# Attention, soft MoE and a gated FFN on one core: the beginning in another order, one streamed weight as two tiles, U and its input in two PSUM banks each

## The chip, the cores and the metric

The kernel runs on one core of a Trainium2 chip. The metric is the device time of one execution in microseconds (us). Three runs of the kernel before gave a median of 526.25 us (526.21 to 527.63).

## The reference

Three layers stand behind each other. The numbers: 4 batches, 8 heads, 768 positions, head width 64; then 3072 tokens of width 512; 8 experts of 4 slots and 1024 hidden units; a last layer of 2048 hidden units.

```python
scores = scale * np.matmul(q, k.transpose(0, 1, 3, 2))
keep = is_global | is_local                     # first n_global keys, and the n_local keys before a position
scores = np.where(keep, scores - slope * dist, -1e9)
x = softmax(scores) @ v                         # tokens (3072, 512)

logits = x @ phi                                # 32 slots
slot_input = softmax(logits, axis=0).T @ x
slot_out[e] = np.maximum(slot_input[e] @ w1[e], 0) @ w2[e]
x = softmax(logits, axis=1) @ slot_out

r = np.maximum(x @ w_in, 0.0)
out = (r * r) @ w_out
```

`n_local` (96) and `n_global` (8) are inputs of the kernel, so the masks are made on the chip.

## The kernel before

Attention goes over 48 units, each a batch, a pair of 128-row query tiles (`tp`, 0 to 2) and a pair of heads (`pr`). A unit i passes through stages that are issued for different units side by side, in an order written out by hand; every engine runs its own instructions in that order. `stage_qk` (L217) makes the scores on TensorE into two PSUM banks (tag `s`, four banks, so two units at once). `stage_max` (L229) adds the mask and takes the row minimum of the negated scores on VectorE. `stage_exp` (L248) is the exponential on ScalarE. `stage_T` (L257) transposes on TensorE, `stage_ev` (L268) copies the transposed block out of PSUM on VectorE or ScalarE, `stage_pv` (L273) multiplies with the values and `stage_x` (L291) copies the result. From unit 4 on a `route` step by step makes the router's logits with `phib`.

A unit's loads are issued on SyncE's queue: `load_qk` (L102) brings 6 blocks of 128 columns (384 KB: two of queries, two of keys, two of the keys that each tile also sees), `load_v` (L108) 4 blocks (256 KB). SyncE issues in program order and waits at a load until the buffer that it overwrites is free, so a load behind it waits as well. The first unit of a batch (`tp` 0) does not use one of the two last blocks: its first tile sees no earlier keys.

The masks are made at the start (L114 to L164). Two tables, R2 (row minus column) and J (column), come as `cmask` from the constants. `n_i`, the two numbers of the input, comes on ScalarE's queue; `n_1` is it as float (L137), a product with `one` spreads it over the partitions (`n_p`, L140), and from that VectorE and GpSimd make `dist` and eight masks, mask h for head h: VectorE mask 0, ScalarE mask 1, GpSimd masks 2 to 7, one after the other. `warm(n, ...)` (L76) is n products of zeros or constants whose result nobody reads.

All weights of the experts together do not fit beside attention. Nine of them are loaded during attention (slots `p0` to `p8`); when attention's buffers are released (L743), the pool `stream` takes their place, with slots `s0`, `s1`, `s2` of 16 KB a partition each. The first streamed weight is `w2_1` in `s0`. Attention's pool `att` gives its first 16 KB a partition to the four `raw` buffers (3 KB each) and then the two `va` buffers (2 KB each, values of half of the units); these make up `s0`. A block named "last" (L753) ends the routing and writes `slotZ`. Then eight times `w1_of` (L805), eight times `w2_of` (L908), with the conversion of the last layer's first weights beside it on VectorE and ScalarE.

Between the experts and the last layer lies a short chain (L1077 to L1101). The slots' result is copied out (`SO`), turned (`pst`), copied in two halves (`soT`: ScalarE the first, VectorE the second), and multiplied with the last layer's first 256 columns (`f0`) in two chunks of 128 (`pu`); each chunk is copied by ScalarE and corrected by VectorE into `U0`. `gemm1` (L997) multiplies U with the spread router shares, and squares; `gemm2` (L1017) makes the output, in five passes over 12 blocks of tokens, with sums kept in `oacc` (in `s0`, `p5`, `p7`).

Of the kernel before, what the change touches and what calls it, by code (L numbers as in the profile page):

```python
# [34 lines left out]
C_ID, C_SI4, C_R2, C_J = 0, 128, 256, 384  # L35
C_W = 512
# [4 lines left out]
def attention_moe_ffn(ctx: ExitStack, tc, qk, vx, nn, phi, w1, w2, w_in, w_out, consts, relw, out):  # L41
# [10 lines left out]
    con = full("con", [P, C_R2])  # L52
# [49 lines left out]
    def load_qk(i):  # L102
        b, tp, pr = units[i]
        r = early.pop("raw", None) if i == 0 else raw_tile(i)
        nc.sync.dma_start(r, qk[b, tp, pr])
        raws[i] = r

    def load_v(i):  # L108
        b, tp, pr = units[i]
        v = early.pop("v", None) if i == 0 else v_tile(i)  # L110
        nc.sync.dma_start(v, vx[b, tp, pr])
        vals[i] = v

    early = {"raw": raw_tile(0), "v": v_tile(0)}  # L114
    cmask = att.tile([P, C_W - C_R2], F32, tag="sm", name="cmask", bufs=3)
    nc.sync.dma_start(cmask, consts[:, C_R2:C_W])
# [3 lines left out]
    nc.sync.dma_start(con, consts[:, 0:C_R2])  # L120
    load_v(0)
    load_qk(2)
    load_qk(3)
# [4 lines left out]
    J = cmask[:, P : 2 * P]  # L128
    mtmp = post.tile([P, 6, P], F32, tag="xb", name="mtmp")
# [4 lines left out]
    V.tensor_tensor(own, own, R2, op=ALU.max)  # L134
    G.tensor_scalar(R1, R2, float(P), None, op0=ALU.add)

    V.tensor_copy(n_1, n_i)  # L137
    warm(10, zero, idle)
    n_p = aps.tile([P, 512], F32, tag="m", name="n_p", bufs=4)
    nc.tensor.matmul(n_p[:, 0:4], lhsT=one, rhs=n_1, start=True, stop=True)  # L140
    V.tensor_copy(n_f, n_p[:, 0:4])
# [16 lines left out]
    for h in range(H):  # L158
        m = mk.tile([P, 3, P], BF16, tag=f"mask{h}", name=f"mask{h}")
        if h == 1:  # L160
            nc.scalar.activation(m, dist, AF.Copy, scale=slope8(h))
        else:
            (G if h else V).tensor_scalar(m, dist, slope8(h), None, op0=ALU.mult)
        masks.append(m)  # L164
# [31 lines left out]
    def load_w(i, part=0, parts=1):  # L196
        name, src, shape, dt = items[i]
        if name == first[0][0]:

            t = slot(SLOTS[i], [P, 2, shape[1]], dt, "raw_0")  # L200
            for j in range(2):
                wt[first[j][0]] = t[:, j, :]
        elif part == 0 and name != first[1][0]:
            wt[name] = slot(SLOTS[i], shape, dt, name)
        n = shape[1] // parts
        ps = slice(part * n, part * n + n)
        nc.sync.dma_start(wt[name][:, ps], src[:, ps])
# [9 lines left out]
    def stage_qk(i):  # L217
        b, tp, pr = units[i]
        r = raws.pop(i)
        sc = [aps.tile([P, 2, 2, P], F32, tag="s", name=f"s{i}_{hh}", bufs=4) for hh in range(2)]  # L220
        for tt in range(2):
            n = width(tp, tt)
            for hh in range(2):
                r0 = hh * D
                rhs = r[r0 : r0 + D, 2 + tt : 3 + tt, :] if n == 1 else r[r0 : r0 + D, 2 + tt : 6 : 2, :]
                nc.tensor.matmul(sc[hh][:, tt, 0:n, :], lhsT=r[r0 : r0 + D, tt, :], rhs=rhs, start=True, stop=True)  # L226
        st[i] = [sc]
# [45 lines left out]
    def stage_pv(i):  # L273
        b, tp, pr = units[i]
        v = vals.pop(i)
        pT = st[i][1]
        o = aps.tile([P, 2, P], F32, tag="s" if i == NU - 1 else "m", name=f"o{i}", bufs=4)
        for tt in range(2):
            n = width(tp, tt)
            for c in range(n):  # L280
                for hh in range(2):
                    nc.tensor.matmul(o[hh * D : hh * D + D, tt, :], lhsT=v[:, tt + 2 * c, hh * D : hh * D + D],  # L282
                                     rhs=pT[:, 2 * tt + hh, c, :], start=c == 0, stop=c == n - 1)
        st[i] = o
# [212 lines left out]
    nc.sync.dma_start(phib, phi)  # L497
# [3 lines left out]
    warm(5, zero, idle)  # L501
# [3 lines left out]
    stage_exp(0, 1)  # L505
    stage_max(1, 0)
    stage_max(1, 1)
    warm(4, zero, idle)
# [4 lines left out]
    for i in range(2):  # L513
        if i:
            stage_T(i)
            stage_max(i + 2, 0)
            stage_ev(i, 0, V.tensor_copy)
        else:
            stage_ev(i, 0, V.tensor_copy)
            stage_max(i + 2, 0)  # L520
        if i:
            stage_exp(i + 1, 0)
            stage_x(i - 1)
        stage_ev(i, 1, nc.scalar.copy)
        stage_exp(i + 1, 1)
        stage_qk(i + 3)
        stage_max(i + 2, 1)
        load_qk(i + 6)
        load_v(i + 3)
        stage_pv(i)  # L530
    stage_exp(3, 0)
# [221 lines left out]
    with tc.block(name="last"):  # L753
# [26 lines left out]
        for c in halves:  # L780
            for h in halves:
                kc = 2 * h + c
                R = slice(2 * h * NS, 2 * h * NS + 2 * NS)
                nc.tensor.matmul(pv[h][:, kc * NS : kc * NS + NS], lhsT=ps[R, c * P : c * P + P], rhs=sden[R], start=False, stop=c == 1)
        for h, eng in ((0, V.tensor_copy), (1, nc.scalar.copy)):
            eng(z[:, :, 2 * h : 2 * h + 2, 0:4], pv[h][:, 2 * h * NS : 2 * h * NS + 2 * NS].rearrange("p (k e s) -> p e k s", e=E, s=4))
# [121 lines left out]
    def w2_of(e):  # L908
        c = wt[f"w2_{e}"]
        for fc in range(8):  # L910
            g = fc % 4
            z = e * 8 * NS + fc * NS
            nc.tensor.matmul(pSO[g * NS : g * NS + NS, :], lhsT=hZ[:, z : z + NS], rhs=c[:, fc, :],  # L913
                             start=e == 0 and fc < 4, stop=e == E - 1 and fc >= 4)
# [82 lines left out]
    def gemm1(q, n, j):  # L997
# [7 lines left out]
        for k in range(K):  # L1005
            c0 = (2 * j + k) * P
            nc.tensor.matmul(ph[:, k, :], lhsT=U[:, c0 : c0 + P], rhs=cst[:, n * TB : n * TB + TB], start=True, stop=True)  # L1007
        rg = ex.tile([P, 2, 2, TB], F32, tag="e", name=f"rg{q}_{n}_{j}", bufs=2)
# [8 lines left out]
    def gemm2(q, n, m):  # L1017
# [7 lines left out]
        o = oacc[k // 8][:, k % 8, :]  # L1025
# [54 lines left out]
    pst = bps.tile([P, 512], F32, tag="sel", name="pst")  # L1080
    pu = bps.tile([P, 512], F32, tag="pu", name="pu0")
# [5 lines left out]
    for kc in range(4):  # L1087
        nc.tensor.matmul(pst[:, kc * P : kc * P + P], lhsT=SO[:, kc * P : kc * P + P], rhs=si4, start=True, stop=True)
    nc.scalar.copy(soT[:, 0:2, :].rearrange("p k s -> p (k s)"), pst[:, 0 : 2 * P])
    V.tensor_copy(soT[:, 2:4, :].rearrange("p k s -> p (k s)"), pst[:, 2 * P : 4 * P])  # L1090
# [5 lines left out]
    for c0 in range(0, WIDTHS[0], P):  # L1096
        c = slice(c0, c0 + P)
        for kc in range(4):
            nc.tensor.matmul(pu[:, c], lhsT=soT[:, kc, :], rhs=f0[:, kc, c], start=kc == 0, stop=kc == 3)
        nc.scalar.copy(U0[:, c], pu[:, c])  # L1100
        V.scalar_tensor_tensor(U0[:, c], U0[:, c].bitcast(F32), odd, pu[:, c], op0=ALU.mult, op1=ALU.add)  # L1101
# [5 lines left out]
    oacc = [slot(t, [P, 8, DM], F32, f"oacc{i}") for i, t in enumerate(("s0", "p5", "p7"))]  # L1107
# [117 lines left out]
def layout(inputs):  # L1225
# [30 lines left out]
    qk = units(qt, kt, seen(kt, 4))  # L1256
    vx = units(vt, seen(vt, 3))
# [5 lines left out]
    con[:, C_R2 : C_R2 + P] = i[:, None] - i[None, :]  # L1263
    con[:, C_J : C_J + P] = i[None, :]
# [36 lines left out]
```

## Time and profile before

| what | us |
|---|---|
| median of three runs | 526.25 |
| the profiled execution | 526.89 |
| its span, first to last instruction | 525.0 |
| TensorE busy | 513.7 (98%) |
| VectorE busy | 381.8 (73%) |
| ScalarE busy | 306.6 (58%) |
| GpSimd busy | 169.1 (32%) |
| attention, to the end of the routing | 0 to about 182 |
| experts | about 182 to 217.6 |
| chain to the last layer | 217.6 to 225.1 |
| last layer | 225.1 to 525.0 |

Matmuls are pipelined in the chip and overlap in the trace, so a TensorE that is busy 98% of the time need not be at its peak: how often it starts a product tells more. An engine's idle time is put down to what ended it. A row of the timeline merges neighbours of one line, so the time of a row divided by its count is near the interval between starts.

### The profile page before, as it was taken

What the parts mean: (1) busy time and instruction counts of PE and PEld (TensorE: products, weight loads), DVE (VectorE), ACT (ScalarE), POOL (GpSimd) and SP (SyncE); (2) the same over time, 40 slices, a digit from 0 to 9 for tenths busy, and PEclk for the clock granted to TensorE, in tenths of its full rate; (3) what the DMA queues carried; (4) which work ended last, traced back from release to release, by engine and by line L of the source; (5) the groups of instructions that cost most, each with busy time, mean ns of one, the idle gap of its engine ahead of it and who ended that gap; (6) DMA issues with size and microseconds to landing.
All of it is one profiled execution on the core that took longest, in us unless ns stands there. A gap on an engine that the chain in (4) does not pass through costs nothing.

```text
span 525.0 us, 10077 instructions
## 1 busy us (share of the span) xinstructions
PE 513.7 (98%) x3628; PEld 393.5 (75%) x3628; DVE 381.8 (73%) x933; ACT 306.6 (58%) x818; POOL 169.1 (32%) x149
## 2 busy tenths in 40 slices
PE   8999999999999999999999999999999999999997
PEld 6777777677767734467787888878888888888886
DVE  5788888787887837588888997967848667445553
ACT  4987878878888303376674655545545446444441
POOL 7000000000000110044655675456554536534441
PEclk9999999999999999999999999999999999999999
DMA  8789999999992999904314030030200000002333
GB/s 292 259 264 318 361 338 311 344 345 316 315 356 70 348 374 423 384 0 162 116 45 160 1 141 21 5 117 0 90 31 1 0 2 0 1 9 113 120 121 121
DMA packets 25978, 89.19 MB, mean 170 GB/s; under 512 B 2882, under 2 KB 3522, under 8 KB 23874
## 3 DMA queue, kind: packets, MB, share of 16 engines
q1 hardware_dynamic: 25776, 88.35, 46.2%
q8 instruction: 30, 0.49, 0.4%
q14 instruction: 26, 0.21, 0.1%
q10 hardware_dynamic: 146, 0.13, 0.1%
HBM read 82.18 MB, written 6.29 MB: 169 GB/s over the span
## 4 chain that ended last, share of the span: by engine, by line
PE 52%; DVE 7%; ACT 1%; issue 1%; POOL 1%; DVEq 0%; POOLq 0%
PE acc L1029 15%; PE acc L1030 14%; PE acc L1031 14%; PE h L1007 4%; PE pSO L913 3%; DVE rg L1012 1%; DVE cvyi L924 1%; DVE cvyi L923 1%; DVE cvyo L924 1%; DVE oacc L1036 1%; PE pre L809 1%; DVE winf L927 1%; DVE oacc L1038 1%; POOL g L1015 1%; ACT rg L1011 1%
## 5 line engine op out<-in xcount | busy, mean ns | idle before, releaser
L1015 POOL TENSOR_TENSOR g<-rg,g 128x512 fp32r<-128x512 f32 (+1 forms) x109 | 135.0, 1241 | 163.5 <-DVE rg L1012 160.7
L1029 PE MATMUL acc<-w,g 128*128 128x512 f32 (+1 forms) x387 | 152.2, 393 | 1.0 <-DVE oacc L1036 1.0
L1031 PE MATMUL acc<-w,g 128*128 128x512 f32 (+1 forms) x387 | 150.6, 389 | 0.7 <-POOL g L1015 0.7
L1030 PE MATMUL acc<-w,g 128*128 128x512 f32 (+1 forms) x387 | 151.3, 391 | 0.0
L1011 ACT ACTIVATE rg<-h 128x512 f32<-128x512 f32 (+1 forms) x109 | 59.6, 546 | 121.9 <-PE h L1007 115.7
L1038 DVE TENSOR_TENSOR oacc<-acc,oacc 128x512 f32<-128x512 f32 x95 | 65.2, 687 | 58.8 <-PE acc L1031 58.8
L254 ACT ACTIVATE sm<-sm,nm 128x256 f32<-128x256 f32 (+1 forms) x192 | 92.8, 489 | 0.3 <-DVE nm L239 0.3
L1031 PEld LDWEIGHTS acc<-w,g 128*128 128x128 f32 x387 | 72.7, 188 | 18.3 <-POOL g L1015 2.8
L1029 PEld LDWEIGHTS acc<-w,g 128*128 128x128 f32 x387 | 72.7, 188 | 17.5 <-ACT rg L1011 2.3
L1030 PEld LDWEIGHTS acc<-w,g 128*128 128x128 f32 x387 | 73.0, 189 | 11.0
L1012 DVE SCALAR_TENSOR_TENSOR rg<-h,rg 128x512 f32<-128x512 f32 (+1 forms) x109 | 67.7, 621 | 16.9 <-ACT rg L1011 16.8
L239 DVE CUSTOM_DVE_ANT_0 sm<-s,mask 128x256 f32<-128x256 f32 (+1 forms) x192 | 66.9, 396 | 3.7 <-ACT sm L254 1.5
L1014 ACT ACTIVATE g<-rg 128x512 fp32r<-128x512 f32 (+1 forms) x109 | 63.4, 582 | 3.5
L226 PE MATMUL s<-raw 64*128 64x256 f32 (+1 forms) x384 | 52.6, 395 | 0.1
L664 POOL TENSOR_TENSOR lh<-lh 128x256 f32<-128x256 f32 x1 | 0.7, 729 | 158.6 <-PE pt L265 158.6
L265 PE MATMUL pt<-con,sm 128*128 128x128 f32 x352 | 45.4, 276 | 1.6 <-ACT pT L271 1.6
L282 PE MATMUL o<-pT,v 128*64 128x128 f32 x704 | 44.4, 277 | 0.2 <-ACT pT L271 0.2
L265 PEld LDWEIGHTS pt<-con,sm 128*128 128x128 f32 x352 | 38.5, 141 | 7.0 <-ACT pT L271 2.8
L282 PEld LDWEIGHTS o<-pT,v 128*64 128x64 f32 x704 | 37.9, 137 | 7.3 <-DVE nm L239 2.2
L226 PEld LDWEIGHTS s<-raw 64*128 64x128 f32 x384 | 31.8, 194 | 14.4 <-DMA v<-in_vx 6.3
L1007 PEld LDWEIGHTS h<-cu 128*128 128x128 f32 x192 | 36.0, 188 | 8.2 <-DVE cu L1101 0.8
L1007 PE MATMUL h<-cu 128*128 128x256 f32 x192 | 40.3, 281 | 0.6 <-DVE cu L1101 0.6
(211 smaller groups left out, 544.5 us busy)
## 6 DMA issues: line engine op xcount, KB each, us to landing
w<-in_w SPq DMA_DIRECT2D x40, 512.0 KB, 6.7
raw<-in_qk SPq DMA_DIRECT2D x48, 384.0 KB, 5.7
v<-in_vx SPq DMA_DIRECT2D x48, 256.0 KB, 4.5
w<-in_w SPq DMA_DIRECT2D x6, 2048.0 KB, 10.1
out_x<-oacc SPq DMA_DIRECT2D x23, 256.0 KB, 2.0
win<-in_w_in SPq DMA_DIRECT2D x2, 2048.0 KB, 9.1
wout<-in_w_out SPq DMA_DIRECT2D x2, 2048.0 KB, 7.9
win<-in_w_in SPq DMA_DIRECT2D x2, 1536.0 KB, 7.3
```

The costliest lines, as they stand in the source:

```text
L226: nc.tensor.matmul(sc[hh][:, tt, 0:n, :], lhsT=r[r0 : r0 + D, tt, :], rhs=rhs, start=True, stop=True)
L239: V.tensor_tensor_reduce(out=sm[:, j, 0:n, :], in0=sc[hh][:, tt, 0:n, :], in1=m[:, 2:3, :] if n == 1 else m[:, 0:2, :], scale=-QK_SCALE, s ...
L254: nc.scalar.activation(sm[:, j, 0:n, :], sm[:, j, 0:n, :], AF.Exp, bias=nm[:, j : j + 1], scale=-1.0, accum_out=chunk_sums(i // NPR)[:, tt ...
L265: nc.tensor.transpose(pp[tt][:, hh, c, :], sm[:, 2 * tt + hh, c, :], ident)
L282: nc.tensor.matmul(o[hh * D : hh * D + D, tt, :], lhsT=v[:, tt + 2 * c, hh * D : hh * D + D], rhs=pT[:, 2 * tt + hh, c, :], start=c == 0, ...
L1007: nc.tensor.matmul(ph[:, k, :], lhsT=U[:, c0 : c0 + P], rhs=cst[:, n * TB : n * TB + TB], start=True, stop=True)
L1012: V.scalar_tensor_tensor(g, ph[:, k0:k1, :], 0.0, r, op0=ALU.max, op1=ALU.mult)
L1015: G.tensor_tensor(g2[:, 1, js, :], g, g2[:, 0, js, :].bitcast(F32), op=ALU.subtract)
L1029: nc.tensor.matmul(pa[:, cs], lhsT=ghi[:, j, ms], rhs=whi[:, j, cs], start=j == 0, stop=False)
L1030: nc.tensor.matmul(pa[:, cs], lhsT=ghi[:, j, ms], rhs=wlo[:, j, cs], start=False, stop=False)
L1031: nc.tensor.matmul(pa[:, cs], lhsT=glo[:, j, ms], rhs=whi[:, j, cs], start=False, stop=j == J - 1)
L1038: V.tensor_tensor(o, pa, o, op=ALU.add)
```

## The change

- The loads of a `tp` 0 unit leave out the block that it does not use: 5 of 6 and 3 of 4 blocks. On the host the last two blocks of a unit change places, so that the unused one is last; the indices in `stage_qk` and `stage_pv` follow.
- R2 and J are made by two `iota` on GpSimd in place of the load of `cmask`. The loads at the start go in the order raw 0, raw 1, raw 2, constants, raw 3, v 0, v 1; `phib` is loaded after the first two units' loop.
- `n_1` is made right after the two first VectorE instructions, 5 in place of 10 `warm` stand before the spread, 4 behind it. The 5 and the 4 `warm` around the first `stage_max` go.
- Mask 3 is made by VectorE between the maxima of unit 0 and unit 1. In the first two units VectorE copies both halves of the transposed block.
- `s0` becomes two tiles, `s0a` and `s0b`, of 8 KB a partition, each with a load of its own; `oacc` is cut in parts of 4 tokens' tiles.
- `pst` gets two banks, and `pu` one bank for each chunk. Four `warm` stand at the end of the block "last", and four between the two first products of `gemm1`.

```diff
-        nc.sync.dma_start(r, qk[b, tp, pr])
+        n = 5 if tp == 0 else 6
+        nc.sync.dma_start(r[:, 0:n], qk[b, tp, pr][:, 0:n])
...
-        nc.sync.dma_start(v, vx[b, tp, pr])
+        n = 3 if tp == 0 else 4
+        nc.sync.dma_start(v[:, 0:n], vx[b, tp, pr][:, 0:n])
...
-    cmask = att.tile([P, C_W - C_R2], F32, tag="sm", name="cmask", bufs=3)
-    nc.sync.dma_start(cmask, consts[:, C_R2:C_W])
+    cmask = att.tile([P, 2 * P], F32, tag="sm", name="cmask", bufs=3)
     load_qk(0)
     early["pT"] = pT_tile(0)
     load_qk(1)
-    nc.sync.dma_start(con, consts[:, 0:C_R2])
+    load_qk(2)
+    nc.sync.dma_start(con, consts)
+    load_qk(3)
     load_v(0)
-    load_qk(2)
-    load_qk(3)
     load_v(1)
...
+    G.iota(R2, [[-1, P]], base=0, channel_multiplier=1, allow_small_or_imprecise_dtypes=True)
+    G.iota(J, [[1, P]], base=0, channel_multiplier=0, allow_small_or_imprecise_dtypes=True)
...
     V.tensor_tensor(own, own, R2, op=ALU.max)
+    V.tensor_copy(n_1, n_i)
     G.tensor_scalar(R1, R2, float(P), None, op0=ALU.add)
-    V.tensor_copy(n_1, n_i)
-    warm(10, zero, idle)
+    warm(5, zero, idle)
     n_p = aps.tile([P, 512], F32, tag="m", name="n_p", bufs=4)
     nc.tensor.matmul(n_p[:, 0:4], lhsT=one, rhs=n_1, start=True, stop=True)
+    warm(4, zero, idle)
...
-        else:
+        elif h != 3:
             (G if h else V).tensor_scalar(m, dist, slope8(h), None, op0=ALU.mult)
...
+        elif SLOTS[i] == "s0":
+            wt[name] = [slot(f"s0{h}", [P, 4, DM], dt, f"{name}{h}") for h in "ab"]
+            for h in range(2):
+                nc.sync.dma_start(wt[name][h], src[:, 4 * h : 4 * h + 4])
+            return
...
     stage_qk(1)
-    nc.sync.dma_start(phib, phi)
...
-    warm(5, zero, idle)
     stage_max(0, 0)
     stage_exp(0, 0)
     stage_max(0, 1)
     stage_exp(0, 1)
+    V.tensor_scalar(masks[3], dist, slope8(3), None, op0=ALU.mult)
     stage_max(1, 0)
     stage_max(1, 1)
-    warm(4, zero, idle)
...
             stage_ev(i, 0, V.tensor_copy)
+            stage_ev(i, 1, V.tensor_copy)
             stage_max(i + 2, 0)
         if i:
             stage_exp(i + 1, 0)
             stage_x(i - 1)
-        stage_ev(i, 1, nc.scalar.copy)
+            stage_ev(i, 1, V.tensor_copy)
...
         stage_pv(i)
+    nc.sync.dma_start(phib, phi)
...
+        warm(4, con, idle)
         for h, eng in ((0, V.tensor_copy), (1, nc.scalar.copy)):
...
+            if q == 0 and n == 0 and k == 0:
+                warm(4, con, idle)
...
-    pst = bps.tile([P, 512], F32, tag="sel", name="pst")
-    pu = bps.tile([P, 512], F32, tag="pu", name="pu0")
+    pst = [bps.tile([P, 512], F32, tag="sel", name="pst0"), pp_of("pst1")]
+    pu = [bps.tile([P, 512], F32, tag=f"pu{j}", name=f"pu0_{j}")[:, 0:P] for j in range(WIDTHS[0] // P)]
...
-    nc.scalar.copy(soT[:, 0:2, :].rearrange("p k s -> p (k s)"), pst[:, 0 : 2 * P])
-    V.tensor_copy(soT[:, 2:4, :].rearrange("p k s -> p (k s)"), pst[:, 2 * P : 4 * P])
+    nc.scalar.copy(soT[:, 0:2, :].rearrange("p k s -> p (k s)"), pst[0][:, 0 : 2 * P])
+    V.tensor_copy(soT[:, 2:4, :].rearrange("p k s -> p (k s)"), pst[1][:, 0 : 2 * P])
...
-            nc.tensor.matmul(pu[:, c], lhsT=soT[:, kc, :], rhs=f0[:, kc, c], start=kc == 0, stop=kc == 3)
-        nc.scalar.copy(U0[:, c], pu[:, c])
-        V.scalar_tensor_tensor(U0[:, c], U0[:, c].bitcast(F32), odd, pu[:, c], op0=ALU.mult, op1=ALU.add)
+            nc.tensor.matmul(pu[c0 // P], lhsT=soT[:, kc, :], rhs=f0[:, kc, c], start=kc == 0, stop=kc == 3)
+        nc.scalar.copy(U0[:, c], pu[c0 // P])
+        V.scalar_tensor_tensor(U0[:, c], U0[:, c].bitcast(F32), odd, pu[c0 // P], op0=ALU.mult, op1=ALU.add)
...
-    oacc = [slot(t, [P, 8, DM], F32, f"oacc{i}") for i, t in enumerate(("s0", "p5", "p7"))]
+    oacc = [slot(t, [P, 4, DM], F32, f"oacc{i}") for i, t in enumerate(("s0a", "s0b"))]
+    for t in ("p5", "p7"):
+        o8 = slot(t, [P, 8, DM], F32, f"oacc_{t}")
+        oacc += [o8[:, 0:4, :], o8[:, 4:8, :]]
```

## Rows read from the trace of the kernel before

**Rows 1.** Windows by stage: busy us and count per engine, PEclk, DMA share, GB/s

```profile
25.00:160.00 135.00, 133.23 (x1453) 100.37 (x1446) 112.58 (x448) 108.93 (x404) 0.00 (x0) 1.00 0.91 321
...
182.00:217.60 35.60, 34.93 (x313) 13.84 (x311) 19.97 (x39) 7.58 (x15) 2.51 (x4) 1.00 0.99 398
...
260.00:515.00 255.00, 254.95 (x1205) 210.10 (x1204) 178.75 (x263) 130.48 (x235) 135.48 (x110) 1.00 0.15 56
```

**Rows 2.** Timeline of the first 9 us: start, duration, engine, line; idle before, its end

```profile
0.74 0.19 POOL L83 MEMSET one<- 1x128 f32 x1 [0.29 <-POOLq L1289]
...
1.06 2.31 PE L79 MATMUL idle<-zero 128*128 128x256 bf16 x10 [1.06 <-DVE zero L74]
...
2.94 0.23 DVE L133 TENSOR_SCALAR mtmp<-cmask 128x128 f32<-128x128 f32 x1 [1.93 <-DMA cmask<-in_consts]
...
3.41 0.17 DVE L137 CAST n<-n_i 1x4 f32<-1x4 int32 x1
...
4.40 2.93 PE L226 MATMUL s<-raw 64*128 64x128 f32 x16
...
6.08 0.36 DVE L163 TENSOR_SCALAR mask<-mtmp 128x384 bf16<-128x384 f32 x1 [0.28 <-POOL mtmp L152]
...
6.13 7.24 POOL L163 TENSOR_SCALAR mask<-mtmp 128x384 bf16<-128x384 f32 x6
6.58 0.29 DVE L239 CUSTOM_DVE_ANT_0 sm<-s,mask 128x128 f32<-128x128 f32 x1
...
7.36 0.42 DVE L239 CUSTOM_DVE_ANT_0 sm<-s,mask 128x256 f32<-128x256 f32 x1
...
8.64 0.29 DVE L239 CUSTOM_DVE_ANT_0 sm<-s,mask 128x128 f32<-128x128 f32 x1 [0.65 <-POOL mask L163]
```

**Rows 3.** Timeline of TensorE alone, 9 to 25 us

```profile
9.30 1.29 PE L226 MATMUL s<-raw 64*128 64x128 f32 x8
10.52 0.87 PE L265 MATMUL pt<-con,sm 128*128 128x128 f32 x6
11.32 0.93 PE L226 MATMUL s<-raw 64*128 64x128 f32 x8
12.18 0.88 PE L282 MATMUL o<-pT,v 128*64 128x128 f32 x12
...
16.73 1.53 PE L265 MATMUL pt<-con,sm 128*128 128x128 f32 x12
...
24.04 1.07 PE L354 MATMUL lt<-xT,phib 64*32 64x256 f32 x16
```

**Rows 4.** All DMA packets from 1.60 to 1.75 us: queue, packets, MB, share

```profile
q10 hardware_dynamic: 2, 0.00, 0.7%
```

**Rows 5.** The load of raw 0, issued at 1.2 us: from issue to landing

```profile
DMA to landing us min/median/max: 3.2/3.2/3.2
```

**Rows 6.** SyncE's wait at the load into s0: total us, times, longest

```profile
SPq L207 <- PE o L282: 5.4, 1, 5.4
```

**Rows 7.** Windows before the load into s0, columns as in Rows 1

```profile
168.00:170.00 2.00, 2.00 (x42) 1.73 (x32) 1.45 (x7) 1.69 (x7) 0.00 (x0) 1.00 0.00 0
```

**Rows 8.** TensorE's weight loads, waits from 202 to 218 us: total, times, longest

```profile
PEld pSO L913 <- DMA w<-in_w: 0.9, 2, 0.6
```

**Rows 9.** Timeline of the chain to the last layer, 219 to 225 us

```profile
219.84 0.42 DVE L1090 COPY soT<-pst 128x256 f32<-128x256 f32 x1 [0.55 <-ACT soT L1089]
...
219.86 1.17 PE L1099 MATMUL pu<-hZ,soT 128*128 128x128 f32 x8
...
221.83 1.16 PE L1099 MATMUL pu<-hZ,soT 128*128 128x128 f32 x8 [0.81 <-DVE cu L1101]
...
223.73 0.38 PE L1007 MATMUL h<-cu 128*128 128x256 f32 x1 [0.62 <-DVE cu L1101]
...
223.96 1.05 PE L79 MATMUL idle<-con 128*128 128x256 bf16 x8
```

**Rows 10.** TensorE's wait at the first expert product: total us, times, longest

```profile
PE pre L809 <- ACT slotZ L786: 0.5, 1, 0.5
```

More of the change, by code (lines that the diff above doesn't have):

```diff
@@ L33 @@
 NBLK = NT // TB
-C_ID, C_SI4, C_R2, C_J = 0, 128, 256, 384
-C_W = 512
+C_ID, C_SI4, C_W = 0, 128, 256
 W_REL = S + (QT - 1) * P
@@ L50, in full @@
         return cp.tile(shape, dt, tag=name, name=name)
-    con = full("con", [P, C_R2])
+    con = full("con", [P, C_W])
     ident = con[:, C_ID : C_ID + P]
@@ L224, in stage_qk @@
                 r0 = hh * D
-                rhs = r[r0 : r0 + D, 2 + tt : 3 + tt, :] if n == 1 else r[r0 : r0 + D, 2 + tt : 6 : 2, :]
+                rhs = r[r0 : r0 + D, 2 + tt : 3 + tt, :] if n == 1 else r[r0 : r0 + D, 2 + tt : 6 - tt : 3 - 2 * tt, :]
                 nc.tensor.matmul(sc[hh][:, tt, 0:n, :], lhsT=r[r0 : r0 + D, tt, :], rhs=rhs, start=True, stop=True)
@@ L281, in stage_pv @@
                 for hh in range(2):
-                    nc.tensor.matmul(o[hh * D : hh * D + D, tt, :], lhsT=v[:, tt + 2 * c, hh * D : hh * D + D],
+                    nc.tensor.matmul(o[hh * D : hh * D + D, tt, :], lhsT=v[:, c * 3 if tt == 0 else 1 + c, hh * D : hh * D + D],
                                      rhs=pT[:, 2 * tt + hh, c, :], start=c == 0, stop=c == n - 1)
@@ L912, in w2_of @@
             z = e * 8 * NS + fc * NS
-            nc.tensor.matmul(pSO[g * NS : g * NS + NS, :], lhsT=hZ[:, z : z + NS], rhs=c[:, fc, :],
+            nc.tensor.matmul(pSO[g * NS : g * NS + NS, :], lhsT=hZ[:, z : z + NS], rhs=c[fc // 4][:, fc % 4, :] if isinstance(c, list) else c[:, fc, :],
                              start=e == 0 and fc < 4, stop=e == E - 1 and fc >= 4)
@@ L1024, in gemm2 @@
         k = n * (TB // P) + m
-        o = oacc[k // 8][:, k % 8, :]
+        o = oacc[k // 4][:, k % 4, :]
         def products(cs):
@@ L1087, in attention_moe_ffn @@
     for kc in range(4):
-        nc.tensor.matmul(pst[:, kc * P : kc * P + P], lhsT=SO[:, kc * P : kc * P + P], rhs=si4, start=True, stop=True)
-    nc.scalar.copy(soT[:, 0:2, :].rearrange("p k s -> p (k s)"), pst[:, 0 : 2 * P])
-    V.tensor_copy(soT[:, 2:4, :].rearrange("p k s -> p (k s)"), pst[:, 2 * P : 4 * P])
+        nc.tensor.matmul(pst[kc // 2][:, kc % 2 * P : kc % 2 * P + P], lhsT=SO[:, kc * P : kc * P + P], rhs=si4, start=True, stop=True)
+    nc.scalar.copy(soT[:, 0:2, :].rearrange("p k s -> p (k s)"), pst[0][:, 0 : 2 * P])
+    V.tensor_copy(soT[:, 2:4, :].rearrange("p k s -> p (k s)"), pst[1][:, 0 : 2 * P])
     spread_ev(2, 1, pp[1])
@@ L1255, in layout, with seen_last_first @@
     vt = v.reshape(B, NPR, 2, QT, P, D).transpose(0, 1, 3, 4, 2, 5).reshape(B, NPR, QT, P, P)
-    qk = units(qt, kt, seen(kt, 4))
-    vx = units(vt, seen(vt, 3))
+    def seen_last_first(a):
+        return np.concatenate([a[..., :-2, :], a[..., -1:, :], a[..., -2:-1, :]], axis=-2)
+    qk = seen_last_first(units(qt, kt, seen(kt, 4)))
+    vx = seen_last_first(units(vt, seen(vt, 3)))
     con = np.zeros((P, C_W), np.float32)
@@ L1262, in layout @@
         con[i, C_SI4 + g * NS + i % NS] = 1
-    con[:, C_R2 : C_R2 + P] = i[:, None] - i[None, :]
-    con[:, C_J : C_J + P] = i[None, :]
     relw = (i[:, None] - np.arange(W_REL)[None, :] + (QT - 1) * P).astype(np.float32)
```

## The prediction

> **What bounds the kernel now.** I first read the windows by stage. TensorE is busy 133.2 of 135 us in attention, 34.9 of 35.6 in the experts and 254.95 of 255 in the last layer, while the next engine, VectorE, has at most 112.6 of those 135 [rows 1]. So TensorE's own order sets the time, and an edit pays only where TensorE waits or has not begun: in the first 10 us, at the end of the experts, and in the chain to the last layer. What is won there should reach the end, since all later stages are TensorE's row of work and none waits for a fixed hour. The DMA queues are the second thing to watch: 0.91 of their time in attention, 0.99 in the experts [rows 1]. I then read these three places instruction by instruction.
>
> The start [rows 2]: `cmask` lands at 2.9 us, VectorE makes two instructions from it, and only behind them, at 3.41, turns n into a float; the masks begin at 6.08, 2.67 later. The first maximum is at 6.58, though the first scores were begun at 4.40. In the second unit VectorE waits 0.65 us for GpSimd, which makes a mask in 7.24 / 6 = 1.2 us. On TensorE nine `warm` stand between the scores of unit 1 and those of unit 2 at 9.30; the first transposes follow at 10.52 and from there to the transposes of units 2 and 3 at 16.73 it is always at work [rows 3]. That row of 6.2 us is the yardstick: the start is worth what the 16.73 moves.
>
> TensorE's clock: the column PEclk says 1.00 everywhere, but ten products of 256 columns at 1.06 us took 2.31 us, 0.21 each, which is 1.2 GHz [rows 2]; eight of the same shape at 223.96 took 1.05, about 0.11 each, which is 2.4 [rows 9]. Eight score products took 1.29 us at 9.30 and the same eight 0.93 at 11.32 [rows 3], so the clock rose near 10 us, after a stretch without a pause that began at 4.40.
>
> **The start, step by step.** (a) GpSimd is free at 0.93 and fills R2, then J. No row shows an iota. The nearest rows are a memset, 0.19, and a mask, 1.2 for three blocks of 128 [rows 2]; I take a third of a mask, 0.4, and keep 0.19 to 1.2. R2 is there at 1.3, J at 1.7. (b) n had landed by 1.75: its two packets are the only ones there [rows 4]. VectorE does its two instructions and reaches n after 0.47 (3.41 less 2.94), at 1.8; the 5 `warm` end at 1.06 + 5 x 0.21 = 2.1, just when the spread wants TensorE. Masks: 1.8 + 2.67, and 0.1 for that meeting, 4.6 in place of 6.08: 1.5 us earlier (0.8 with the slow iota). (c) Raw 0 is first in SyncE's queue, issued at 0.75 where `cmask` was. It took 3.2 us with 128 KB ahead of it [rows 5], so it lands by 3.95, rather sooner with 320 KB and nothing ahead. The 4 `warm` behind the spread end at about 3.5; the scores of unit 0 begin at 3.5 to 3.95, I take 3.8. Units 0 and 1 take 2.7 at the low clock (the 2.93 of rows 2 less its last tail): to 6.5. (d) Unit 0's maxima end at 7.78 - 1.5 = 6.3, which frees the banks for unit 2. Its scores start at 6.5 in place of 9.30, and the transposes, 1.3 to 1.4 later, at 7.9 in place of 10.52. Raw 2, third of three loads of 320 KB, has then had some 5 us. (e) Mask 3 costs VectorE 0.36 and takes away the 0.65: another 0.3. (f) From the transposes on TensorE needs 6.2 us at 2.4 GHz. If the clock is low until about 10, the first two groups (10.52 to 12.18, 1.7 us) take about 0.9 more: the mark falls at 7.9 + 6.2 + 0.9 = 15.0, 1.7 us earlier than 16.73. With the clock up by 7.9 it falls at 14.1, 2.6 earlier, and 3.2 if it is up by 6.5. TensorE now has no pause from the spread on, so I take 2.2.
>
> What hides the rest: the copies moved from ScalarE to VectorE cost it up to 2 x 0.42 each by the 256-wide copy [rows 9]; VectorE then has about 4.7 us of maxima and copies in the 5 us before the scores of unit 5. If it is late there, up to 0.8 us goes. `phib` moves behind ten loads and is issued after v 4, at about 11; it is wanted at 24.04 [rows 3], about 22 afterwards, and loads of this queue landed in 3.2 us with the queue full [rows 5]: hidden by several us. v 0 moves behind raw 2, the constants and raw 3, and is wanted only after the first transposes are copied. Leaving out blocks spares 16 units x 128 KB = 2 MB; no TensorE wait in attention hangs on a load, so I count nothing for it.
>
> **The first streamed weight.** SyncE waits 5.4 us at this load for the last unit that reads a `va` buffer, while the DMA engines move nothing [rows 6, 7]. `s0a` covers 8 KB of the `raw` buffers alone, which are free when the load is reached, so 1 MB goes into that hole. The later weights then come up to a MB's time earlier; 1 MB at the experts' 398 GB/s [rows 1] is 2.6 us. But TensorE waits there only 0.9 us in total for weights, twice [rows 8], on one of four column groups while others run: I count 0.4 (0 to 0.9). After that TensorE's own products bound the stage.
>
> **U and its input.** VectorE's half of `soT` waited 0.55 us for ScalarE's half of the same bank, and the first chunk of `pu` began at 219.86. With two banks ScalarE's half no longer waits for all of `pst`, and the chunk is held by the transposes ahead of it: I take 0.3 earlier, 219.6. Chunk 2 stood until 221.83 for VectorE's correction of chunk 1. In its own bank it follows chunk 1 after eight products at about 0.12: 220.57, so 1.26 earlier. From its start to the second product of U is 1.90 (221.83 to 223.73) and stays: that product falls at 222.5, and with it squares and output products [rows 9]. The 4 `warm` ahead of it take 0.44 and lie in the wait for chunk 2's correction. I take 1.3 (0.8 to 1.6). The 4 `warm` of the block "last" take 0.44 in a wait of 0.5 [rows 10]: nothing, at worst 0.2.
>
> **The sum.** 2.2 + 0.4 + 1.3 = 3.9 us. The profiled execution took 526.89 (span 525.0 and 1.9 around it), so it becomes 523.0; the median was 526.25, 0.64 below it, and becomes 522.4.
>
> **Rivals.** First, the clock rises late. The change takes nine `warm` out of the stretch in which it rose. For: the transposes stand now where these were. Against: TensorE has other products in their place and no pause from the spread on. The Trainium skill says on the page "TensorE: Matmul & The Clock Gate", Part 1, that the throttled state is the default and activity releases it, and that the point varies from run to run; the rows agree on the two levels. By that rule the fillers were what earned the clock, and taking them out would eat the start's 2.2 us. Price, from the rows: each us at 1.2 GHz after 7.9 costs about 0.45. Rising at 13.5 leaves 0.1 of the start's gain: 524.4. At 17 it has cost 1.4, and the whole change gives 0.3: 526.0. From about 17.5 on the kernel is slower than before; at 21 by over 0.3%, 527.8 or more.
>
> Second, the start's gain is lost later: attention then is paced by loads (0.91 of the queues' time [rows 1]) or by ScalarE. Against: no wait of TensorE on a load, and 2 MB fewer. It leaves 0.4 + 1.3: 524.5.
>
> Third, the change doesn't do what it says for `s0`: its first half still waits for a `va` reader, or the weights were not late for lack of that MB. 0.4 less: 522.8.
>
> **How the numbers follow.** Forecast, the clock up by 10.5 us: 0.66, giving 3.3 to 4.9 less, 521.3 to 522.9. The clock between 10.5 and 17: 0.18, 522.9 to 526.0. Later: 0.05. Paced elsewhere: 0.08. `s0` without effect: 0.03. The range takes in a fast iota and an early clock below, and the second rival and most of the late clock above: 520.8 to 524.8. About 0.3% (1.6 us) is what a measurement can tell from no change. Faster by more: the forecast, 0.11 of the late clock (up to about 14), 0.05 of the second rival and the third: 0.85. Within: 0.12. Slower: 0.03.
>
> **What would show it.** Right: n turned at about 1.8 us, masks at 4.6, transposes of units 2 and 3 at 14 to 15, the routing's end as much earlier; DMA busy from 166 to 170; no wait for weights at the experts' end; second chunk of `pu` right behind the first, U's second product about 2.9 us after the first chunk began, in place of 3.9. Wrong: eight score products still 1.29 us long beyond 11 us; an iota over 1.2; a TensorE wait on a load in attention; the mark at 16.73 moved but attention's end not.

## The result: 522.05 us, 4.9 us less

| | before | after |
|---|---|---|
| median of four runs of each (us) | 526.94 (526.21 to 528.25) | 522.05 (521.95 to 522.18) |
| the profiled execution / its span | 526.89 / 525.0 | 522.18 / 520.4 |

The ratio is 0.9905, with a 95% interval of 0.9881 to 0.9928. The span is 4.59 us shorter. The first table follows it through the kernel, from one row of TensorE to the next. Each column is one profile.

| from ... to (first instruction of each) | before | after | difference |
|---|---|---|---|
| start ... the mark, transposes of units 2 and 3 | 16.73 | 14.38 | -2.35 |
| ... first product with `phib` | 7.32 | 6.95 | -0.36 |
| ... router's logits of the last chunk | 148.25 | 148.08 | -0.17 |
| ... first product of the experts | 12.70 | 12.88 | +0.17 |
| ... first product with w2 | 17.45 | 17.45 | 0 |
| ... spread behind the experts | 15.18 | 14.69 | -0.49 |
| ... first output product | 7.45 | 5.98 | -1.47 |
| ... end | 299.89 | 299.98 | +0.09 |

**The start.** The timeline of the kernel after, as in [rows 2] (start, duration, engine, line, operation; in brackets the idle time before and its end):

```profile
0.98 0.23 POOL L129 IOTA cmask<- 128x128 f32 x1
...
1.99 0.16 DVE L137 CAST n<-n_i 1x4 f32<-1x4 int32 x1 [0.18 <-DMA n_i<-in_nn]
...
4.73 0.36 DVE L166 TENSOR_SCALAR mask<-mtmp 128x384 bf16<-128x384 f32 x1 [0.28 <-POOL mtmp L155]
...
5.43 0.29 DVE L247 CUSTOM_DVE_ANT_0 sm<-s,mask 128x128 f32<-128x128 f32 x1 [0.34 <-PE s L234]
...
6.34 0.50 PEld L234 LDWEIGHTS s<-raw 64*128 64x128 f32 x2 [0.38 <-DVE nm L247]
```

An iota takes 0.23 us. n is turned at 1.99, where VectorE now waits 0.18 for its landing; the masks begin at 4.73 in place of 6.08. The first maximum, at 5.43, no longer waits for a mask but for scores. The load of the weights for unit 2's scores waits 0.38 for VectorE at 6.34, but TensorE still has unit 1's products then. TensorE alone, as in [rows 3]:

```profile
3.75 4.49 PE L234 MATMUL s<-raw 64*128 64x128 f32 x24
8.17 0.88 PE L273 MATMUL pt<-con,sm 128*128 128x128 f32 x6
8.98 0.93 PE L234 MATMUL s<-raw 64*128 64x128 f32 x8
...
14.38 1.53 PE L273 MATMUL pt<-con,sm 128*128 128x128 f32 x12
...
16.91 1.53 PE L290 MATMUL o<-pT,v 128*64 128x128 f32 x24
...
21.33 0.68 PE L362 MATMUL lt<-xT,phib 64*32 64x256 f32 x16
```

The scores begin at 3.75 and the transposes at 8.17. Eight score products take 0.93 us at 8.98, so the clock is up by then; before, the eight at 9.30 took 1.29 [rows 3].

**The streamed weights.** SyncE's queue; each row is an issue with its count:

```profile
162.49 0.33 SPq L209 DMA_DIRECT2D w_1a<-in_w  x1
167.28 0.33 SPq L209 DMA_DIRECT2D w_1b<-in_w  x1
172.03 12.56 SPq L215 DMA_DIRECT2D w<-in_w  x3
```

And two windows of it (busy time and count of each engine, then PEclk, DMA share, GB/s):

```profile
165.00:167.00 2.00, 2.00 (x46) 1.73 (x32) 1.56 (x8) 1.69 (x8) 0.00 (x0) 1.00 0.91 344
167.00:169.00 2.00, 2.00 (x23) 1.83 (x18) 0.90 (x2) 1.87 (x7) 0.00 (x0) 1.00 0.52 123
```

The hole of [rows 7], 0 GB/s, is filled, and the waits of [rows 8] are not listed any more: no weight load of TensorE has a DMA put down as what it waited for. The end of the experts hangs on the weights all the same: the last one lands at 213.39, the four loads that want it begin at 213.44, and the spread follows at 214.42. Before, these are 216.60, 216.64 and 217.63.

**The chain to the last layer**, as in [rows 9]:

```profile
216.23 0.42 DVE L1101 COPY soT<-pst 128x256 f32<-128x256 f32 x1
...
216.35 1.96 PE L1110 MATMUL pu<-hZ,soT 128*128 128x128 f32 x16
...
218.52 0.61 PE L78 MATMUL idle<-con 128*128 128x256 bf16 x4
219.05 0.39 PE L1016 MATMUL h<-cu 128*128 128x256 f32 x1
...
220.40 0.46 PE L1040 MATMUL acc<-w,g 128*128 128x512 f32 x1
```

VectorE's half of `soT` waits for nothing, both chunks of `pu` are one row of 16, and U's second product stands 2.70 us behind the first chunk (3.87 before).

### The profile page after: what moved, and what is told of

Read it like the earlier page. It is cut to its first block, busy times and chain, and to the rows that moved or that the text cites. A ratio compares the mean times of both kernels' runs of the same rounds, so it can differ in the third digit from the quotient of the medians.

```text
span 520.4 us, 10077 instructions
## 1 busy us (share of the span) xinstructions
PE 511.6 (98%) x3626; PEld 392.9 (76%) x3626; DVE 383.4 (74%) x936; ACT 305.9 (59%) x816; POOL 168.4 (32%) x150
## 4 chain that ended last, share of the span: by engine, by line
PE 53%; DVE 7%; ACT 1%; issue 1%; POOL 1%; DVEq 0%; POOLq 0%
PE acc L1040 15%; PE acc L1041 14%; PE acc L1042 14%; PE h L1016 4%; PE pSO L922 3%; DVE rg L1023 1%; DVE cvyi L933 1%; DVE cvyi L932 1%; DVE cvyo L933 1%; PE pre L818 1%; DVE winf L936 1%; DVE oacc L1049 1%; POOL g L1026 1%; ACT rg L1022 1%; DVE cvyo L932 1%
## 5 line engine op out<-in xcount | busy, mean ns | idle before, releaser
L1049 DVE TENSOR_TENSOR oacc_p<-acc,oacc_p 128x512 f32<-128x512 f32 x63 | 43.4, 688 | 45.3 <-PE acc L1042 45.2
```

## The experiments

Each is set against the kernel before on the same chip: the two medians, then the ratio with its 95% interval, which is an estimate of its own and not the quotient of the medians. "Mark" is always the start of the transposes of units 2 and 3.

### Each part alone

**`u_banks`**: the kernel before with two banks for `pst` and for `pu`, without the four `warm` of `gemm1`.

```diff
-    pst = bps.tile([P, 512], F32, tag="sel", name="pst")
-    pu = bps.tile([P, 512], F32, tag="pu", name="pu0")
+    pst = [bps.tile([P, 512], F32, tag="sel", name="pst0"), pp_of("pst1")]
+    pu = [bps.tile([P, 512], F32, tag=f"pu{j}", name=f"pu0_{j}")[:, 0:P] for j in range(WIDTHS[0] // P)]
```

> The kernel before with the two banks for pst and one bank for each chunk of pu, nothing else. My theory: the second chunk of pu follows the first at once, the first output product of the last layer falls at about 223.7 in place of 225.08, the total is 1.3 us (0.8 to 1.6) lower. Rival: the chain is held by something else (the 8 warm products, VectorE's two corrections) and gives it back: 0 to 0.5 us.

525.55 us against 526.99, a ratio of 0.9958 (0.9928 to 0.9987). From the spread to the first output product it takes 5.98 us, to the hundredth what the whole change takes, and 7.45 before. So the 1.47 us is the banks' alone. This profile's mark is 17.25, 0.52 later than before; before unit 1's scores TensorE waits 0.46 for a load there.

**`s0_halves`**: the kernel before with `s0` in two tiles.

```diff
+        elif SLOTS[i] == "s0":
+            wt[name] = [slot(f"s0{h}", [P, 4, DM], dt, f"{name}{h}") for h in "ab"]
+            for h in range(2):
+                nc.sync.dma_start(wt[name][h], src[:, 4 * h : 4 * h + 4])
+            return
```

> The kernel before with s0 as two tiles and two loads, nothing else. My theory: the first half's load is issued at about 164.8 us in place of 170.17 and fills the hole in the DMA queues; the wait of TensorE's weight loads for the experts' weights (0.9 us before) goes, and the transposes behind the experts begin at 217.1 to 217.3 in place of 217.63: 0.4 us lower in total. Rival: the weights were not late for lack of that MB, the wait stays at 0.9 and the total is the same.

526.79 against 526.99, 1.0005 (0.9984 to 1.0026). The first half is issued at 164.41, 5.8 us earlier, and yet the weight loads wait for DMAs as before (view of waits, 199 to 225 us: total, times, longest):

```profile
PEld pSO L918 <- DMA w<-in_w: 1.2, 2, 0.8
```

The loads do what they say, and the stretch from w2 to the spread takes 15.40 us, not less than the 15.18 before. This profile's clock happened to rise early: its eight score products at 8.71 took 0.93 us, with the old beginning, and its mark is 15.93.

**`start_alone`**: the change with `s0` whole, one bank each, and without the four `warm` of "last" and of `gemm1`.

```diff
-        warm(4, con, idle)
...
-            if q == 0 and n == 0 and k == 0:
-                warm(4, con, idle)
...
-    pu = [bps.tile([P, 512], F32, tag=f"pu{j}", name=f"pu0_{j}")[:, 0:P] for j in range(WIDTHS[0] // P)]
+    pu = bps.tile([P, 512], F32, tag="pu", name="pu0")
...
```

> The changed kernel with s0 whole again, pst and pu in one bank each and without the two added groups of 4 warm: the new beginning and the shorter loads alone. My theory: the transposes of units 2 and 3 begin near 14.4 us (16.73 before), all later marks keep this 2.4 us and gain a few tenths where ScalarE's lag ended a wait near 20 us: 2.4 to 2.9 us lower in total, so that the three parts add up to the whole. Rival: attention is paced by loads or ScalarE and gives the start's gain back: under 1 us.

524.96 against 526.99, 0.9959 (0.9938 to 0.9979): 2.0 us lower in the median, where I expected 2.4 to 2.9. In the profile the mark is at 13.93; its execution took 523.59. The ten runs lie in two groups, 523.19 to 524.82 and 525.11 to 525.78. Each run comes with its mean granted clock, and that is 0.999 or 1.0 in the first five and 0.996 or 0.997 in the second five. What may lie behind it is seen in `trimmed`, below.

### The clock and the fillers

**`fillers_back`**: the change with the 5 and the 4 `warm` around the first maximum put back.

```diff
+    warm(5, zero, idle)
     stage_max(0, 0)
...
+    warm(4, zero, idle)
```

> The changed kernel with the 5 and the 4 warm products put back around the first maxima. My theory: they only stand in the way; unit 2's scores begin at about 8.2 us in place of 6.3, the first transposes at about 9.0 in place of 8.17, the transposes of units 2 and 3 near 15.2 in place of 14.38: 0.8 us slower than the changed kernel if the clock rises when it does there (near 8 us), 1.7 if it rises near 10. Rival (fillers earn the clock): with them the clock rises earlier than near 8 us and the total is the same or lower than the changed kernel's.

522.87 against 526.99, 0.9932 (0.9910 to 0.9955). TensorE alone:

```profile
6.59 2.10 PE L78 MATMUL idle<-zero 128*128 128x256 bf16 x9
8.62 0.93 PE L234 MATMUL s<-raw 64*128 64x128 f32 x8
9.48 0.87 PE L273 MATMUL pt<-con,sm 128*128 128x128 f32 x6
...
15.68 1.53 PE L273 MATMUL pt<-con,sm 128*128 128x128 f32 x12
```

Nine products take the 2.1 us in which the scores of unit 2 could run, and the clock is up at 8.62, no sooner to be seen than in the change. The mark is 1.30 later (0.8 was expected). In the new beginning the fillers earn nothing.

**`fillers_out`**: the kernel before without the same nine.

```diff
-    warm(5, zero, idle)
     stage_max(0, 0)
...
-    warm(4, zero, idle)
```

> The kernel before without the 5 and the 4 warm products around the first maxima, nothing else. My theory: unit 2's scores then wait only for their data, landed at 8.3 us, in place of 9.30, and the transposes of units 2 and 3 begin about 0.9 earlier for the same clock: near 15.8 if it rises at 10. Rival (fillers earn the clock): the rise comes later than 10.1 us, each us of delay costs 0.2 to 0.45, and the mark stays at 16.7 or falls later.

529.24 against 527.26, 1.0020 (0.9996 to 1.0044); the interval takes in no change. TensorE alone:

```profile
6.20 1.66 PE L226 MATMUL s<-raw 64*128 64x128 f32 x8 [0.30 <-DMA raw<-in_qk]
9.21 1.65 PE L226 MATMUL s<-raw 64*128 64x128 f32 x8 [1.36 <-DMA raw<-in_qk]
10.79 1.54 PE L265 MATMUL pt<-con,sm 128*128 128x128 f32 x6
12.26 1.65 PE L226 MATMUL s<-raw 64*128 64x128 f32 x8
...
18.53 1.53 PE L265 MATMUL pt<-con,sm 128*128 128x128 f32 x12
```

The same edit in the old beginning has the mark at 18.53: 1.80 later than before, against my theory and for the rival. With the fillers the mark lies at 16.73, 15.93 (`s0_halves`) and 17.25 (`u_banks`), so it is later than in all three. The pause of 1.36, which the fillers covered, is now bare, and the clock is still at 1.2 GHz at 12.26, where the eight take 1.65; before, they took 0.93 at 11.32 [rows 3]. The pause of 0.30 lies ahead of the fillers' place and is not the edit's: `u_banks` has one of 0.46 there, and with the fillers behind it eight score products took 0.93 at 10.19. The Trainium skill says on the page "TensorE: Matmul & The Clock Gate", Part 1, that the throttled state is the default and activity releases it; the trace agrees. It also says there that the ramp is worth under 1% of a typical kernel's span; the 1.80 by which two ramps differ here is 0.34% of 525.0, which agrees too, but is more than a third of what this whole change brings. Three of the ten runs took 526.17 to 527.36, the others 528.85 to 530.32; the profile is of the latter, and how the three went is open. It also waits 3.8 us for weights behind the experts, which no start explains.

**`pause`**: the change without the four `warm` behind the spread.

```diff
     nc.tensor.matmul(n_p[:, 0:4], lhsT=one, rhs=n_1, start=True, stop=True)
-    warm(4, zero, idle)
```

> The changed kernel without the 4 warm products behind the spread of n, so that TensorE stands still from about 2.7 us until the first scores' data land at about 3.75. My theory: what TensorE does without a pause before the scores brings the clock up early; with the pause it rises about 2 us later than the 6 to 8.6 us seen with this beginning, near 10, and the transposes of units 2 and 3 begin 0.4 to 0.9 later than 14.4, total 0.4 to 0.9 above the changed kernel. Rival: the point of the rise is a matter of the run and not of these 4 products; rise between 6 and 8.6, mark and total as in the changed kernel.

522.86 against 527.26, 0.9917 (0.9886 to 0.9947). TensorE alone:

```profile
3.60 4.59 PE L233 MATMUL s<-raw 64*128 64x128 f32 x24 [0.77 <-DMA raw<-in_qk]
8.11 1.54 PE L272 MATMUL pt<-con,sm 128*128 128x128 f32 x6
...
15.07 1.53 PE L272 MATMUL pt<-con,sm 128*128 128x128 f32 x12
```

A pause of 0.77 us at 2.8, the same products behind it, and the first six transposes take 1.54 in place of 0.88: the mark is 0.69 later, at the same start of the transposes. That is what I expected if work without a pause raises the clock, whether anybody reads its result or not, but it is not shown. The profile of `copies_back` has the change's beginning as far as these transposes, without the pause, and there they take 1.23 and the mark is 14.80, only 0.27 ahead of this one. The four runs, 522.04 to 523.27, lean the same way (521.95 to 522.18 for the change), and no more.

**`fill_gap`**: five in place of those four, to close the last gap of 0.2 us before the scores.

```diff
-    warm(4, zero, idle)
+    warm(5, zero, idle)
```

> The changed kernel with 5 in place of 4 warm products behind the spread of n, which fills the pause of 0.2 us that TensorE makes before the first scores. My theory: with no pause left the clock rises at about 6 us in most runs and the transposes of units 2 and 3 begin near 14.0: total 0 to 0.4 below the changed kernel, and its runs closer together. Rival: the rise still falls anywhere between 6 and 8.6 us; no difference.

522.17 against 527.72, 0.9895 (0.9875 to 0.9914); the mark is 14.56, the transposes begin at 8.35 with 0.88 for six. The gap was no cause: without it the clock is up at the same place, against what I expected. Nor do other rows tell why it came earlier in some profiles: with the same instructions at the beginning as the change the marks are 13.93 in `start_alone`, 13.93 in `s1_halves`, 14.05 in `whole_loads`, 14.07 in `whole_s0`, 14.46 in `trimmed` and 14.80 in `copies_back`. They differ by how early the scores of unit 2, or the first transposes, get faster.

### The streamed weights

**`whole_s0`**: the change with `s0` as one tile. **`s1_halves`**: the change with `s1` in two tiles as well.

```diff
-        elif SLOTS[i] == "s0":
+        elif SLOTS[i] in ("s0", "s1"):
```

> The changed kernel with s0 as one tile and one load again. The forecast's theory: the two loads gave the 0.5 us between the experts' first w2 product and the transposes behind them (15.18 before, 14.69 after), so it is 15.2 here with two waits for weights of 0.9 in total. Rival, after s0_halves: the last weight lands 29.1 to 29.9 us after the issue of the load into p0, however early s0 came, and the difference is the spread of that number from run to run: 14.7 to 15.4 here, and no difference in total that can be told.

> The changed kernel with s1, the second streamed weight's slot, as two tiles and two loads as well; its first half covers buffers that are free some 3.5 us before those of the second. Theory A (the queue's backlog from s1 on sets the stream's end, 41.3 to 41.9 us after s1's issue so far): the last weight lands 1 to 3 us earlier against the experts' first product, no wait for weights, 14.4 to 14.6 us from the first w2 product to the transposes behind it, at most 0.5 us gained. Theory B (the release of later slots sets it): the last weight lands 29.1 to 29.9 us after the issue into p0 as before, 14.6 to 15.1 us, nothing gained.

`whole_s0`: 522.17 against 527.26, 0.9912 (0.9883 to 0.9942). `s1_halves`: 522.38 against 527.72, 0.9898 (0.9878 to 0.9918). Neither differs from the change. The whole `s0` is issued at 166.99, 4.5 us later than the change's first half; no wait for a weight is listed all the same, and the stretch from w2 to the spread takes 14.63 us (14.69 with halves). With `s1` in halves all of `s0` and `s1` has landed by 178.35, where `s1` alone lands at 180.00 in the change, and here a wait is listed:

```profile
PEld pSO L922 <- DMA w<-in_w: 0.8, 2, 0.5
```

The table shows why early bytes are worth nothing. The load into `p0` waits for the first expert's products, which free it, and behind it come eight more, two of them for the last layer.

| us | before | s0_halves | after | whole_s0 | s1_halves |
|---|---|---|---|---|---|
| first byte of `s0` asked for | 170.17 | 164.41 | 162.49 | 166.99 | 162.05 |
| first product of the experts | 185.00 | 184.03 | 182.28 | 182.00 | 181.84 |
| load into `p0` issued | 186.97 | 186.00 | 184.26 | 183.97 | 183.81 |
| last streamed weight lands | 216.60 | 215.85 | 213.39 | 213.05 | 213.41 |
| from the load into `p0` to this landing | 29.63 | 29.85 | 29.13 | 29.08 | 29.59 |
| spread begins | 217.63 | 216.88 | 214.42 | 214.08 | 214.43 |
| listed wait for weights | 0.9 | 1.2 | 0 | 0 | 0.8 |

The load into `p0` is issued 2.0 us behind the first product of the experts (3.55 in `trimmed`, below, where these products ran slower), the last weight comes 29.1 to 29.9 us after it, whatever came ahead, and the spread begins 1.03 behind the last weight. These 1.03 stand in all fourteen profiles, whether a wait is listed or not, so the last weight sets the end of the experts each time. In the 29 us the DMA engines have no hole left to fill, as the windows from that issue to that landing show, before and after (columns as above):

```profile
186.97:216.60 29.63, 29.46 (x267) 11.23 (x259) 16.77 (x30) 6.92 (x13) 2.51 (x4) 1.00 0.99 405
184.26:213.39 29.13, 28.96 (x265) 11.23 (x259) 16.76 (x30) 6.76 (x13) 2.51 (x4) 1.00 1.00 403
```

The time to the last landing varies from profile to profile, and not with `s0` or `s1`: it is 30.1 in `copies_back` and 31.4 in `fillers_out`, which touch none of these loads. Why is open.

### The smaller edits

**`whole_loads`**: the change with all blocks loaded.

```diff
-        n = 5 if tp == 0 else 6
+        n = 6
...
-        n = 3 if tp == 0 else 4
+        n = 4
```

> The changed kernel with all 6 and all 4 blocks loaded in every unit, 2 MB more. My theory: nothing in the start but a landing of the first scores' data some tenths later (3.9 in place of 3.73), and the stretch from the first product with phib to the first logits of the last chunk, 148.08 us in the kernels with short loads and 148.24 in those with whole ones, is 148.24 here: 0.2 to 0.4 slower in total. Rival: the short loads are what lets the new beginning work (unit 2's or 3's data late): 1 us or more slower.

522.78 against 527.26, 0.9930 (0.9906 to 0.9954). The stretch from the `phib` product to the last logits is 148.11 us, with 2 MB more, and 148.08 in the change: the shorter loads bring nothing there. Its six runs lie at 521.97 to 522.09 and at 523.47 to 524.07, three and three; what the second three are is open.

**`copies_back`**: the change with ScalarE copying the second half in the first two units again.

```diff
-            stage_ev(i, 1, V.tensor_copy)
+        stage_ev(i, 1, nc.scalar.copy)
```

> The changed kernel with ScalarE again copying the second half of the transposed block in the first two units, as before the change. My theory: ScalarE's row of exponentials then runs behind, the transposes of units 2 and 3 keep near 14.1 to 14.4, but the stretch from them to the first product with phib is 7.3 us again (7.31 before, 6.95 with the change): 0.4 to 0.5 slower. Rival: the copies are hidden on either engine, 6.95 and no difference.

523.42 against 527.72, 0.9916 (0.9895 to 0.9937). From the mark to the `phib` product it takes 7.32 us, as before, not 6.95. TensorE alone, and behind it the same place in the kernel before:

```profile
17.33 1.09 PE L290 MATMUL o<-pT,v 128*64 128x128 f32 x16
18.57 0.66 PE L290 MATMUL o<-pT,v 128*64 128x128 f32 x8 [0.15 <-ACT pT L279]
```

```profile
19.25 1.09 PE L282 MATMUL o<-pT,v 128*64 128x128 f32 x16
20.50 0.66 PE L282 MATMUL o<-pT,v 128*64 128x128 f32 x8 [0.15 <-ACT pT L271]
```

In both, the products with the values break for a copy that ScalarE has late; in the change 24 of them run through, at 16.91. Here ScalarE was behind, not VectorE. The rest of this profile's loss is the mark (14.80, its clock rising late, before any of these copies) and a wait of 1.7 us for weights, as scattered as in the table above. So 0.37 is what the edit accounts for, where I expected 0.4 to 0.5.

**`trimmed`**: the change with `s0` whole and without the four `warm` in "last" and in `gemm1`.

```diff
-        warm(4, con, idle)
...
-            if q == 0 and n == 0 and k == 0:
-                warm(4, con, idle)
```

> The changed kernel with s0 as one tile, without the 4 warm products at the end of the block last and without the 4 between the two first products of U. My theory: these three parts of the change bring nothing. The stretch from the last chunk's first logits to the experts' first product is 12.70 us again in place of 12.87; what that gives is waited for at the weights; first output product after the experts' transposes 5.98 as in the change; total within 0.3 us of the changed kernel. Rival: the fillers in front of the experts speed up their products or the s0 halves matter after all: 0.5 us or more slower.

523.75 against 527.72, 0.9927 (0.9899 to 0.9955): worse than the change, against what I expected. From the spread to the first output product it takes 5.97 us without the four of `gemm1`: those do nothing. But from the first to the second expert layer it takes 19.15 us, and 17.45 in every other profile. Windows of this kernel, columns as above, and its row of TensorE; then the row of the change:

```profile
180.00:182.00 2.00, 1.74 (x20) 1.49 (x16) 0.61 (x4) 0.13 (x1) 0.00 (x0) 1.00 0.85 311
182.00:184.00 2.00, 1.79 (x12) 0.73 (x16) 1.88 (x3) 0.13 (x2) 0.00 (x0) 0.60 1.01 426
184.00:186.00 2.00, 2.00 (x14) 0.54 (x8) 1.13 (x2) 0.80 (x1) 0.00 (x0) 0.55 0.61 258
186.00:188.00 2.00, 2.00 (x24) 0.79 (x20) 1.26 (x2) 0.00 (x0) 0.00 (x0) 1.00 0.74 164
...
182.21 12.20 PE L812 MATMUL pre<-w,slotZ 128*32 128x512 f32 x96 [0.47 <-ACT slotZ L789]
```

```profile
181.57 0.61 PE L78 MATMUL idle<-con 128*128 128x256 bf16 x4
182.28 10.51 PE L818 MATMUL pre<-w,slotZ 128*32 128x512 f32 x96
```

PEclk falls to 0.60 and 0.55 from 182 to 186 us, right behind the wait of 0.47 for `slotZ`, and 96 products take 1.69 more. From 150 us on no longer wait of TensorE stands ahead of it. The four `warm` fill that wait: in the change 0.10 is left of it. The same wait of 0.47 stands in the profile of `start_alone`, whose clock did not fall, so it does not bring the fall each time, and makes it possible at most. The runs bear it out as far as they go: of the 35 of kernels with these four none has a mean granted clock under 0.999; of 92 without them (48 of the kernel before, 44 of experiments) 11 have 0.996 or 0.997. Among kernels with the new beginning it is none of 35 against seven of 14, five of them in `start_alone`, where those five are 1.8 us longer in the median (525.38 against 523.59). Only this one was traced: that the other ten fell at the same place is argued, not shown, and why `start_alone` has so many is open.

## Why the prediction was right

The forecast took 3.9 us off the profiled execution of 526.89; it lost 4.71. The mechanism of the start and of the chain was right, one step failed, and two that were counted at nothing were not nothing. That the sum comes so near is in part luck, as the first and the third point say.

- **Start, 2.2 forecast, 2.35 measured.** (a) iota 0.4, measured 0.23, near the low end of 0.19; it did not matter, since n, at 1.99 and not 1.8, was held by its landing. (b) Masks at 4.6, measured 4.73. (c) Scores at 3.8, measured 3.75. (d) Transposes at 7.9, measured 8.17: in this profile all 24 score products ran at the low clock, 4.49 us; where it rose during them (3.86 in `start_alone`) the transposes begin at 7.51. (f) The mark between 14 and 15, measured 14.38, which is 8.17 and the yardstick of 6.2. How much of it is the order and how much the clock is seen beside `s0_halves`, where the old beginning had its clock up by 8.71 too: its mark is 15.93, so with like clocks the order brings 1.55, and the earlier clock the other 0.80, by this one profile. The mark varies with the clock and with when the loads land, 15.93 to 17.25 in three profiles of the old beginning and 13.93 to 14.80 in seven of the new, so it is luck that this pair comes within 0.15 of the forecast; the two medians are 2.66 apart.
- **The late clock, 0.18 and 0.05, did not come.** The rival had a ground: in the old beginning, by the one profile of `fillers_out`, the nine `warm` earned the clock. But what counted against it held: in the new beginning other products stand in their place, and `fillers_back` is later with the nine, not earlier. That a pause ahead of these products would cost something is likely from `pause`, not shown.
- **`s0`, 0.4 forecast, nothing measured: this step failed.** The third rival, at 0.03, was the true one, in its second form. The hole is filled as said, but "the later weights then come up to a MB's time earlier" is wrong: the load into `p0` waits for the first expert's products, 2.0 us behind the first of them with or without the early half, and from there to the last landing the DMA engines are busy all the time. `s0_halves`, `whole_s0` and `s1_halves` end alike. Wrong too is that behind the 0.4 "TensorE's own products bound the stage": the last weight does, with 1.03 us to the spread in every profile. I had read that the DMA engines stood idle, and not asked whether a queue stood behind the hole to move up. The hole was also shorter than the wait of 5.4 us: from 166 to 168 us the engines still moved 96 GB/s. The 0.49 that the stretch from w2 to the spread did lose is the 0.50 by which the last weight followed sooner on the load into `p0` (29.13 for 29.63), and lies within what the same loads vary by: the stretch takes 14.63 to 15.67 in kernels with the four `warm` in "last". That it comes near the 0.4 is luck.
- **U and its input, 1.3 forecast, 1.47 measured**, with the first chunk 0.30 earlier in `u_banks` (0.3 forecast) and chunk 2 right behind it. The Trainium skill, on the page "PSUM — Partial Sum Buffer", section "Summary: rules for kernel authors", tells to read one bank while the matmul writes another; the row of 16 in place of two of 8 agrees.
- **Copies on VectorE, counted as hidden with a loss of up to 0.8, brought 0.36**, and perhaps 0.12 of the 0.17 in the rest of attention, since `copies_back` has 148.20 there and the change 148.08. I priced what VectorE would pay and left out that ScalarE paid before: its row had the wait of 0.15 in the stretch behind the mark.
- **The four `warm` of "last", nothing or at worst 0.2, cost 0.17**. By the runs above they also seem to guard against a fall of the clock that cost 1.7 where it was traced; the forecast had that nowhere. The shorter loads: nothing, as forecast.
- **Lost later, 0.08**: no. The mark's 2.35 is still there at the last logits, with 0.53 more.

Part by part: 2.35 and 0.53 up to the last logits, less 0.17, and 0.49 and 1.47 behind, less 0.09 at the end, are 4.58.

## What to carry to other kernels

A transfer brought forward into a hole pays only if the last one lands sooner for it; before counting its time, look at what releases the loads behind it, and from which of them on the queue has no hole. A stage can hang on a landing though no wait is listed: compare the landing with the first use over several profiles. A filler product is worth keeping where TensorE would pause, not where real products can stand: ask of each what stands in its place when it goes. And one profile of a beginning is not enough to price a few tenths, if the clock rises at another point in the next. When two engines copy out of one bank, or a second group of products waits for the reader of the first, a bank each turned 7.45 us into 5.98.

## What the runs showed of the hardware

- An iota of 128 x 128 on GpSimd took 0.23 us, little more than a memset of one row (0.19, [rows 2]).
- The clock can fall back to 1.2 GHz in the middle of the kernel behind a wait of only 0.47 us, in a stretch that shows TensorE busy 1.74 of 2 us; at 186 us it was at 2.4 again. It cost 1.7 us on 96 products (`trimmed`).
- With one and the same beginning, the first transposes began at 7.51 to 8.24 us and the mark lay at 13.93 to 14.80, from one profile to the next, by how early the clock rose.
- One and the same row of nine loads, with the DMA engines busy 0.97 to 1.01 of the time, took 29.1 to 31.4 us from the first issue to the last landing.
